# An attention and MLP kernel: two rows of a weight product in float32, group scores merged, zeros moved to the front

## The chip, the cores and the metric

The kernel runs on one core of a Trainium2 chip. The metric is the device time of one execution in microseconds (us), the median of several runs. A core has these engines: TensorE (PE; its weight loads are listed as PEld), VectorE (DVE), ScalarE (ACT), GpSimd (POOL) and SyncE (SP), which issues most transfers.

## What is computed

```python
q_d = q.reshape(B, H, Sd, factor, D).mean(axis=3)      # k_d, v_d alike; factor 4
out_up = np.repeat(sm_attn(q_d, k_d, v_d), factor, axis=2)
mask = np.abs(pos[:, None] - pos[None, :]) < factor
scores = np.where(mask, scale * np.matmul(q, k.transpose(0, 1, 3, 2)), -1e9)
out_local = softmax(scores) @ v
x = (out_up + out_local).transpose(0, 2, 1, 3).reshape(B * S, H * D)
return ((x @ w1) * (x @ w2)) @ w3 @ w_out
```

B = H = 8, S = 576, D = 64; x is 4608 x 512, w1 and w2 are 512 x 1024, w3 is 1024 x 1024, w_out 1024 x 512. The four weights arrive as 64-bit floats, everything else is float32.

## The kernel before

**The weight product.** The last two weights are multiplied once on the chip (`fold`): w3 @ w_out, 1024 x 512, stays in `wphl`. w3 is cut into blocks of 128 rows of the inner dimension, j = 0 to 7, and two halves mq of four output blocks m. A block row j needs block j of w_out (`out_weight`) and block (j, mq) of w3 (`block`); `product(m, j)` adds their product to the sum of m, which stays in PSUM until j = 7, and `keep` stores it.

**Split float32.** A float32 product is computed by `three` as three float32r instructions: high x high, high x low, low x high. Every operand is therefore split into a high part (a copy by ACT) and a low part (a subtraction by DVE). A weight block goes through `words` and `parted`: SP loads the 64-bit words (L337, 512 KB); ACT makes the upper part (L344); the low bits come from ACT (L352) or DVE (L356, "shift"); DVE joins them (L359, "join"); ACT copies the high half (L371); DVE subtracts (L375).

**Attention.** Batches 0 and 1 do the local attention on PE in groups of 16 pooled positions: for each unit n (a third of a batch) `group_scores` computes scores of two quads of heads (L769, tile `se_ps`), adds the band mask (L780), takes the maximum (L789, L790), exponentials on ACT (L793) and normalises; `group_values` multiplies by v. Batches 2 to 7 do it on DVE and ACT (`unit`). The pooled attention of each batch (`pooled`, `quad`) gives scores `s_ps`, transposes `t_ps` and values `o_ps` on PE. `pooled_sums` loads q and k in four phases for batches 0 and 1, sums them and turns q into natural order.

**The chunks.** Two units form a chunk of 384 rows of x. `moe(c)` computes, for eight blocks f of 128 features, the two gate products (tile `pab`, 24 instructions for each), multiplies them (ACT and DVE, then split into `gh`, `gl`), and three down products (`acc`, three instructions each) with `wphl`.

**What sets the order.** All work is a list of tasks with an engine, a cost and dependencies. The table ORDER names, for each engine, the order of its tasks; `Plan.order` interleaves the engines by those costs, and each engine then runs its own queue strictly in that order. A ring (`R[...]`) of n buffers makes a task wait until the one n places before has been used up; the small PSUM tiles of the scores and transposes share one ring of three ("g").

At the start, `warm` multiplies zeros (`still`, L412) on PE, 20 times, before the first product.

Of the kernel before, what the change touches and what calls it, by code (L numbers as in the profile page):

```python
# [20 lines left out]
FAC = 4  # L21
# [31 lines left out]
            g=2, o=2, ab=2, acc=1, ps=3, p=1, pt=1, oup=2, vs=1, qks=1, x=2, s=3, gs=3, q4=2, k4=2, qn=2, vw=4, se=4, pte=1, xf=1)  # L53
# [4 lines left out]
WARM = 20  # L58
# [41 lines left out]
    ),  # L100
    DVE=(
# [62 lines left out]
    ),  # L164
)

LOWS = dict(early=('ACT', 'ACT', 'DVE'), late=('ACT', 'DVE'))


class Ring:  # L170
# [91 lines left out]
def mm_us(n):  # L262
    return n * 0.43e-3 + 0.0095
# [10 lines left out]
def tile_attention_moe(ctx: ExitStack, tc: tile.TileContext, q, kw, vw, qk4, v4, w1, w2, w3, wout, edge, out):  # L274
# [115 lines left out]
    def fold():  # L390
# [66 lines left out]
        for mq in range(2):  # L457
            for j in range(NF):
                if not mq:
                    out_weight(j)  # L460
# [763 lines left out]
```

## Time and profile before

| | |
|---|---|
| median of three runs | 750.81 us (749.66 to 752.25) |
| profiled execution: span, first to last instruction | 747.4 us |
| PE busy | 729.4 us (98%) |
| DVE busy | 617.8 us (83%) |
| ACT busy | 544.3 us (73%) |
| POOL busy | 108.2 us (14%) |
| HBM read, written | 80.26 MB, 9.44 MB |

The span is that of one profiled execution; its own whole time is not listed beside it, and the median of the runs lies 3.4 us above the span. Busy times are unions over the span. A PE instruction's end is modelled and reaches into the next one, so the pace is read from starts. Names with numbers such as `wo_302` are tiles; before, a line of `three` is L312, L313 or L314, after the change L316, L317 or L318.

### The profile page before, as it was taken

The numbers are of one execution on the slowest core, as the hardware profiler recorded it, in microseconds if no ns is written. First come the engines' busy times: TensorE is split into PE (matmuls) and PEld (weight loads), VectorE is DVE, ScalarE is ACT, GpSimd is POOL, SyncE is SP. The second block draws the span as 40 slices with busy tenths as digits, with TensorE's granted clock in tenths as the row PEclk, the third lists the DMA queues.
The fourth block names the chain that finished last, engine by engine and source line by source line (L and its number), as shares of the span: only waits on it lengthen the run. The fifth ranks groups of instructions, "written<-read, shape, count | busy, mean of one in ns | idle before, by whom it ended". The sixth has DMA issues, their size and how long they took to land.

```text
span 747.4 us, 15049 instructions
## 1 busy us (share of the span) xinstructions
PE 729.4 (98%) x5352; PEld 658.2 (88%) x5352; DVE 617.8 (83%) x1088; ACT 544.3 (73%) x2157; POOL 108.2 (14%) x139
## 2 busy tenths in 40 slices
PE   4999999999999999999999999999999999999997
PEld 3677888789998989999898998999899999999996
DVE  6988996557999999989999998999989988885212
ACT  5999878566897878778878886877887875853211
POOL 2020002210112210212222110221120110010000
PEclk9999999999999999999999999999999999999999
DMA  8998765746767877396577674668666354233101
GB/s 257 322 261 262 236 204 105 131 84 194 151 143 175 167 171 189 61 241 165 89 168 220 120 184 150 100 197 176 141 145 164 63 152 127 63 66 56 43 0 43
DMA packets 51999, 111.91 MB, mean 150 GB/s; under 512 B 5060, under 2 KB 19396, under 8 KB 51924
## 3 DMA queue, kind: packets, MB, share of 16 engines
q0 software_dynamic: 14592, 38.94, 30.9%
q1 hardware_dynamic: 37044, 71.74, 29.0%
q8 instruction: 42, 0.69, 0.4%
q10 hardware_dynamic: 288, 0.27, 0.1%
q14 instruction: 33, 0.27, 0.1%
HBM read 80.26 MB, written 9.44 MB: 120 GB/s over the span
## 4 chain that ended last, share of the span: by engine, by line
PE 96%; DVE 2%; DMA 1%; issue 0%; ACT 0%; SPq 0%
PE pab L312 19%; PE pab L314 18%; PE pab L313 18%; PE acc L312 9%; PE acc L313 9%; PE acc L314 9%; PE o_ps L553 2%; PE accw L312 2%; PE s_ps L592 2%; PE t_ps L631 2%; PE accw L313 2%; PE accw L314 2%; PE se_ps L769 1%; PE oe_ps L812 1%; PE te_ps L739 1%; DMA q<-in_qk_dram 1%
## 5 line engine op out<-in xcount | busy, mean ns | idle before, releaser
L942 ACT ACTIVATE pv<-kv,s 128x64 f32<-128x64 f32 x432 | 115.3, 338 | 15.2 <-DVE s L919 8.9
L894 ACT ACTIVATE junk<-pr 128x64 f32<-128x64 f32 x432 | 110.2, 255 | 17.3 <-DVE pr L884 8.0
L884 DVE TENSOR_TENSOR pr<-q_t,kv 128x768 f32<-128x768 f32 x126 | 115.8, 950 | 0.6 <-ACT junk L894 0.3
L312 PE MATMUL acc<-wphl,gh 128*128 128x512 f32 x288 | 113.6, 395 | 0.0
L314 PE MATMUL acc<-wphl,gl 128*128 128x512 f32 x288 | 112.9, 392 | 0.0
L313 PE MATMUL acc<-wphl,gh 128*128 128x512 f32 x288 | 112.8, 392 | 0.0
L958 POOL DMA_DIRECT2D xl<-pv x54 | 46.5, 862 | 370.2 <-DVE xl L960 271.3
L1047 DVE TENSOR_TENSOR a<-pab,a 128x384 f32<-128x384 f32 x96 | 53.1, 553 | 45.1 <-PE pab L314 35.2
L1045 ACT COPY a<-pab 128x384 f32<-128x384 f32 x96 | 45.3, 471 | 60.4 <-PE pab L314 56.3
L897 DVE TENSOR_REDUCE s<-pr 128x12 f32<-128x768 f32 x90 | 83.8, 946 | 0.4
L894 ACT ACTIVATION_READ_ACCUMULATOR junk<-pr 128x1 f32 x432 | 81.1, 188 | 0.0
L1052 ACT CAST gh<-a 128x384 fp32r<-128x384 f32 x96 | 48.9, 510 | 38.5 <-PE acc L313 27.5
L1054 DVE TENSOR_TENSOR gl<-a,gh 128x384 fp32r<-128x384 f32 x96 | 52.7, 552 | 26.8 <-ACT gh L1052 26.5
L950 DVE TENSOR_TENSOR pv<-kv,s 128x768 f32<-128x768 f32 x72 | 67.7, 951 | 0.4
L312 PE MATMUL pab<-xh,w1a 128*128 128x384 f32 x192 | 65.7, 342 | 0.0
L312 PE MATMUL pab<-xh,w2a 128*128 128x384 f32 x192 | 65.4, 340 | 0.0
L312 PE MATMUL pab<-xh,wo 128*128 128x384 f32 x192 | 65.3, 340 | 0.0
L312 PE MATMUL pab<-xh,wb 128*128 128x384 f32 x192 | 65.2, 339 | 0.0
L314 PE MATMUL pab<-xh,wo 128*128 128x384 f32 x192 | 64.5, 336 | 0.0
L314 PE MATMUL pab<-xh,wb 128*128 128x384 f32 x192 | 64.5, 336 | 0.0
L314 PE MATMUL pab<-xh,w1a 128*128 128x384 f32 x192 | 64.5, 336 | 0.0
L313 PE MATMUL pab<-xl,wo 128*128 128x384 f32 x192 | 64.5, 336 | 0.0
(126 smaller groups left out, 1766.6 us busy)
## 6 DMA issues: line engine op xcount, KB each, us to landing
xl<-pv POOLq DMA_DIRECT2D x54, 384.0 KB, 4.2
raw<-in_w_dram SPq DMA_DIRECT2D x32, 512.0 KB, 5.3
qks<-in_qk_dram POOLq DMA_DIRECT2D x18, 576.0 KB, 7.3
kv<-in_kw_dram SPq DMA_DIRECT2D x18, 576.0 KB, 4.1
kv<-in_vw_dram SPq DMA_DIRECT2D x18, 576.0 KB, 5.5
q_t<-in_q_dram SPq DMA_DIRECT2D x18, 384.0 KB, 3.3
vs<-in_v_dram POOLq DMA_DIRECT2D x24, 256.0 KB, 5.7
out_dram<-o_sb SPq DMA_DIRECT2D x23, 256.0 KB, 2.8
```

The costliest lines, as they stand in the source:

```text
L312: nc.tensor.matmul(out_ps, lhsT=lh, rhs=rh, start=first, stop=False)
L313: nc.tensor.matmul(out_ps, lhsT=lh, rhs=rl, start=False, stop=False)
L314: nc.tensor.matmul(out_ps, lhsT=ll, rhs=rh, start=False, stop=last)
L884: (nc.gpsimd if o in share["qk_pool"] else nc.vector).tensor_tensor(out=T[o], in0=T["q"], in1=T["k"][:, o * D:o * D + nq].rearrange("p (t ...
L894: nc.scalar.activation(out=junk, in_=T[o][:, t], func=AF.Copy, accum_out=T["s"][:, t, o:o + 1])
L897: reds.append(add("DVE", dve_us(nq), lambda o=o: nc.vector.tensor_reduce(out=T["s"][:, :, o], in_=T[o], op=ALU.add, axis=AX.X), [tp], uses ...
L942: nc.scalar.mul(out=T["pv", o][:, tt], in_=T["v"][:, (tt + o) * D:(tt + o + 1) * D], mul=T["s"][:, tt, o:o + 1])
L950: nc.vector.tensor_tensor(out=T["pv", o], in0=T["v"][:, o * D:o * D + nq].rearrange("p (t d) -> p t d", d=D), in1=T["s"][:, :, o].unsqueez ...
L958: t = add("Pool", 0.9, lambda o=o: nc.gpsimd.dma_start(out=T["x"], in_=T["pv", o], accum_op=ALU.add), [t, tm], uses=[hx, h], late=dma_us(1 ...
L1047: tg = add("DVE", dve_us(CT), lambda f=f: nc.vector.tensor_tensor(out=straight(T["a", f]), in0=turned(T["p", 1, f]), in1=straight(T["a", f ...
L1052: nc.scalar.copy(out=T["gh", f], in_=T["a", f])
L1054: tl = add("DVE", dve_us(CT), lambda f=f: nc.vector.tensor_tensor(out=T["gl", f], in0=T["a", f], in1=T["gh", f].bitcast(F32), op=ALU.subtr ...
```

## The change

1. `WHOLE = (0, 1)`: the block rows j = 0 and 1 of the weight product are not split. Their four w3 blocks and two w_out blocks stay float32 (`whole`), and `product` multiplies them with one float32 instruction instead of three float32r ones. The two w_out blocks live in the `oup` buffers, and are the first weights to be loaded.
2. `group_scores` handles both quads of a unit in one task: 24 products, masks of 432, a maximum of 864 elements; `pooled_sums` loads q and k of two head pairs at a time (`q4` has one buffer).
3. The band mask is moved by four products with the identity on PE (`banding`, L686) and one DVE copy, not by eight DVE copies; with the zeros, now 26, it stands first on PE.
4. `NORM_DVE = (0,)`: for batch 0 the pooled probabilities are normalised by DVE (two operations a quad), not by ACT.
5. ORDER is new for all engines.

```diff
-            g=2, o=2, ab=2, acc=1, ps=3, p=1, pt=1, oup=2, vs=1, qks=1, x=2, s=3, gs=3, q4=2, k4=2, qn=2, vw=4, se=4, pte=1, xf=1)
+            g=2, o=2, ab=2, acc=1, ps=3, p=1, pt=1, oup=2, vs=1, qks=1, x=2, s=3, gs=3, q4=1, k4=2, qn=2, vw=4, se=2, pte=1, xf=1)
-WARM = 20
+WARM = 26
+NORM_DVE = (0,)
+WHOLE = (0, 1)
...
+    def whole(src, parts, place, take=()):
+        T, ld, tx, h = words(src, place, list(take), "early", parts)
+        early.append(tx)
+        return T, [tx], h
...
     def out_weight(j):
...
+        if j in WHOLE:
+            T, wo_ready[j], wo_held[j] = whole(wout[j].unsqueeze(1), 1, lambda: work.tile([128, KT * SD], F32, name="oup", bufs=BUFS["oup"])[:, :DM], [R["oup"]])
+            wo_whole[j] = T
+            return
...
         def block(j, mq):
...
+            if j in WHOLE:
+                xs[j, mq] = whole(src, 4, lambda: pools["early"].tile([128, nw], F32, name="wx", bufs=BUFS["early_wx"]), [R["early_wx"]])
+                return
...
-                three(accs[m], T["h"][:, cs], T["l"][:, cs], wo[0][:, j], wo_low[:, j], j == 0, j == NF - 1)
+                if j in WHOLE:
+                    nc.tensor.matmul(accs[m], lhsT=T["x"][:, cs], rhs=wo_whole[j]["x"], start=j == 0, stop=j == NF - 1)
+                else:
+                    three(accs[m], T["h"][:, cs], T["l"][:, cs], wo[0][:, j], wo_low[:, j], j == 0, j == NF - 1)
...
+        if b in NORM_DVE:
+            for par in range(2):
+                no.append(add("DVE", dve_us(nt * width[par]), lambda par=par: nc.vector.tensor_tensor(out=T["of"][par][:, :, :width[par]], in0=T["of"][par][:, :, :width[par]], in1=wide_(T["sm"][:, :nt, par], width[par]), op=ALU.mult), [rs], uses=[hg, hp]))
+        for par, i in slots if b not in NORM_DVE else ():
...
+    def banding():
...
+                for i, (at, n) in enumerate(((0, 2), (1, 2))):
+                    nc.tensor.matmul(T["b"][rows, 2 * i:2 * i + n], lhsT=ident[rows, rows], rhs=masks[0][rows, half, at:at + n].rearrange("p i s f -> p (i s f)"), start=True, stop=True)
...
-    def group_scores(b, j, qd, starts):
+    def group_scores(b, j, starts):
...
+                U["s", par] = ps.tile([128, 2, NG, GK], F32, tag="g", name="se_ps", bufs=BUFS["ps"])
+            for qd in range(2):
+                for g, (q0, k0) in enumerate(starts):
...
-        sc, b0, b1 = add("PE", 2 * NG * mm_us(2 * GK) + SWITCH, score, l4, take=[R["ps"], R["ps"]], uses=h4)
+        sc, b0, b1 = add("PE", 4 * NG * mm_us(2 * GK) + SWITCH, score, sum(l4s, []), take=[R["ps"], R["ps"]], uses=sum(h4s, []))
...
+    for j in WHOLE:
+        out_weight(j)
```

The queue of PE at its start, before (`se_ps` are group scores, `still` the zeros, `accw` the sums of the weight product):

```order
L769 MATMUL se_ps<-k_153,qn 64x72 x12
L412 MATMUL accw_197<-still 128x128 x20
L312 MATMUL accw_197<-wo,w_178 128x512
L313 MATMUL accw_197<-wphl,w_178 128x512
L314 MATMUL accw_197<-wo,w_178 128x512
```

and with the change (`b_ps` is the band mask, L456 the float32 product, `s_ps` the pooled scores):

```order
L686 MATMUL b_ps<-xh_97,ident 64x144 x4
L429 MATMUL accw_146<-still 128x128 x26
L456 MATMUL accw_146<-oup,wx 128x512
L456 MATMUL accw_147<-oup,wx 128x512
L456 MATMUL accw<-oup,wx 128x512 x2
L456 MATMUL accw_148<-oup,wx 128x512
L796 MATMUL se_ps<-k_191,qn 64x72 x12
L796 MATMUL se_ps<-k_193,qn 64x72 x12
L456 MATMUL accw_148<-oup,wx 128x512
L456 MATMUL accw_146<-oup,wx 128x512
L456 MATMUL accw_147<-oup,wx 128x512
L796 MATMUL se_ps<-k_191,qn 64x72 x12
```

The zeros no longer stand behind the first group scores; eight float32 products and the scores of two units stand ahead of the first split product. The other eight float32 products stand behind the first half, in three places between split products.

The queue of DVE from the first group masks on, with the change (`wx` joins, `raw` shift, `emx` maximum, `wphl` and `w_320` the low halves for the first split product):

```order
L807 TENSOR_TENSOR se<-se_ps,band 128x432 x2
L363 SCALAR_TENSOR_TENSOR wx<-wx,raw 128x512
L360 TENSOR_SCALAR raw<-raw 128x512
L817 TENSOR_REDUCE emx<-se 128x12
L818 TENSOR_SCALAR emx<-emx 128x12
L363 SCALAR_TENSOR_TENSOR wx<-wx,raw 128x512
L380 TENSOR_TENSOR wphl<-wx,wo 128x512
L807 TENSOR_TENSOR se<-se_ps,band 128x432
L363 SCALAR_TENSOR_TENSOR wx<-wx,raw 128x512
L380 TENSOR_TENSOR w_320<-wx,w_320 128x512
```

Before, the low halves of the first split product stand ahead of the first group masks:

```order
L1149 COPY band<-xh_97 64x72 x8
L375 TENSOR_TENSOR wphl<-wx,wo 128x512
L375 TENSOR_TENSOR w_178<-wx,w_178 128x512
L700 TENSOR_TENSOR qks<-k_153 128x288
L780 TENSOR_TENSOR se<-se_ps,band 128x216 x2
```

So the masks of both units, and with them the PE tasks that they wait for, now stand on DVE ahead of the halves that the first split product needs.

PE at the last group scores before the gates, before:

```order
L769 MATMUL se_ps<-k_153,qn 64x72 x12
L312 MATMUL accw<-wo,w_911 128x512
L313 MATMUL accw<-wphl,w_911 128x512
L314 MATMUL accw<-wo,w_911 128x512
L769 MATMUL se_ps<-k_272,qn 64x72 x12
L312 MATMUL pab<-xh_984,w1a 128x384
```

and with the change:

```order
L316 MATMUL accw_582<-wo,w_784 128x512
L317 MATMUL accw_582<-wphl,w_784 128x512
L318 MATMUL accw_582<-wo,w_784 128x512
L796 MATMUL se_ps<-k_191,qn 64x72 x12
L796 MATMUL se_ps<-k_193,qn 64x72 x12
L316 MATMUL pab<-xh_881,w1a 128x384
```

The two tasks of a unit have become neighbours; the other three units behind this place change in the same way. From the first gate on, the down products stand in 172 unbroken runs between gate products, before in 103.

## Rows read from the trace of the kernel before

**Rows 1.** The page's part 4: the chain that ended last, by engine.
```profile
PE 96%; DVE 2%; DMA 1%; issue 0%; ACT 0%; SPq 0%
```

**Rows 2.** Waits of PE from 28 us to the end.
```profile
PE se_ps L769 <- DVE se L780: 0.7, 1, 0.7
```

**Rows 3.** Timeline of PE, start: start us, us, engine, line, operation, tiles, shape [idle before].
```profile
11.10 1.03 PE L769 MATMUL se_ps<-k,qn 64*64 64x72 f32 x24 [11.10 <-DMA k<-in_qk_dram]
12.06 7.17 PE L412 MATMUL accw<-still 128*128 128x128 f32 x40
19.00 0.48 PE L312 MATMUL accw<-wo,w 128*128 128x512 f32 x1
...
21.11 0.40 PE L313 MATMUL accw<-wphl,w 128*128 128x512 f32 x1
22.21 0.50 PE L314 MATMUL accw<-wo,w 128*128 128x512 f32 x1 [0.70 <-DVE w L375]
```

**Rows 4.** Timeline of POOL, its last masks.
```profile
4.57 1.31 POOL L1146 TENSOR_SCALAR_AFFINE_SELECT xh<-xh 128x72 f32<-128x72 f32 x3
```

**Rows 5.** Zeros of L412 by stretch: us, busy us (records) of PE and PEld, PEclk, DMA, GB/s.
```profile
12.10:17.20 5.10, 5.10 (x24) 5.10 (x25) 1.00 0.74 233
```

**Rows 6.** Timeline of PE around a lone task of group scores.
```profile
30.00 0.40 PE L313 MATMUL accw<-wphl,w 128*128 128x512 f32 x1
30.23 0.39 PE L314 MATMUL accw<-wo,w 128*128 128x512 f32 x1
30.55 0.97 PE L769 MATMUL se_ps<-k,qn 64*64 64x72 f32 x24
31.45 0.50 PE L312 MATMUL accw<-wo,w 128*128 128x512 f32 x1
31.80 0.39 PE L313 MATMUL accw<-wphl,w 128*128 128x512 f32 x1
```

**Rows 7.** Timeline of DVE between 13 and 19 us.
```profile
13.45 0.67 DVE L780 TENSOR_TENSOR se<-se_ps,band 128x216 f32<-128x216 f32 x2
...
14.25 0.42 DVE L356 TENSOR_SCALAR raw<-raw 128x512 int32<-128x512 int32 x1
14.59 0.30 DVE L683 TENSOR_TENSOR qks<-qks,q 128x144 f32<-128x144 f32 x1
14.81 0.69 DVE L359 SCALAR_TENSOR_TENSOR wx<-wx,raw 128x512 int32<-128x512 int32 x1
15.41 0.60 DVE L789 TENSOR_REDUCE emx<-se 128x6 f32<-128x432 f32 x1
15.92 0.30 DVE L683 TENSOR_TENSOR qks<-qks,q 128x144 f32<-128x144 f32 x1
...
17.09 0.94 DVE L700 TENSOR_TENSOR qks<-qks,k 128x288 f32<-128x288 f32 x2
17.95 0.68 DVE L375 TENSOR_TENSOR wphl<-wx,wo 128x512 fp32r<-128x512 f32 x1
18.55 0.69 DVE L359 SCALAR_TENSOR_TENSOR wx<-wx,raw 128x512 int32<-128x512 int32 x1
```

**Rows 8.** All engines from 3 to 13 us; the last two columns are DMA share and GB/s.
```profile
3.00:13.00 10.00, 1.90 (x28) 1.77 (x29) 5.22 (x16) 4.24 (x7) 2.88 (x8) 1.00 1.04 353
```

**Rows 9.** Timeline of PE: three places of the run.
```profile
51.50 0.40 PE L312 MATMUL accw<-wo,w 128*128 128x512 f32 x1
...
83.65 0.44 PE L312 MATMUL pab<-xh,w1a 128*128 128x384 f32 x1
...
741.14 0.39 PE L314 MATMUL acc<-wphl,gl 128*128 128x512 f32 x1
...
741.82 0.39 PE L314 MATMUL acc<-wphl,gl 128*128 128x512 f32 x1
```

**Rows 10.** Timeline of PE: a lone run of three down instructions.
```profile
181.84 0.39 PE L312 MATMUL acc<-wphl,gh 128*128 128x512 f32 x1
...
182.53 0.34 PE L312 MATMUL pab<-xh,wo 128*128 128x384 f32 x1
```

More of the change, by code (lines that the diff above doesn't have):

```diff
@@ L299, in tile_attention_moe @@
     nc.vector.memset(soft[:, :, SD:KEYS[1]], 0.0)
-    bands = []
+    bands, masks, band_sb = [], [], []
     gates = [[wpool.tile([128, KT, 2, 512], F32R, name=f"w{w}a"), None, None] for w in (1, 2)]
@@ L363, in tile_attention_moe @@
     wo_ready, wp_ready, g_ready = {}, {}, {}
+    wo_whole, wo_held = {}, {}
     wo_low = wphl[:, NF // 2:].rearrange("p f h n -> p (f h) n")
@@ L445, in product @@
             else:
-                t = add("PE", 3 * mm_us(DM), prod, deps, uses=[h, held[m]])
+                t = add("PE", 3 * mm_us(DM), prod, deps, uses=[h, held[m]] + wh)
             last[m] = t
@@ L458, in fold @@
             for j in range(NF):
-                if not mq:
+                if not mq and j not in WHOLE:
                     out_weight(j)
@@ L653, in pooled_sums, with turn @@
     @plan.named
+    def banding():
+        T = {}
+        def turn():
+            T["b"] = ps.tile([128, NG + 1, GK], F32, tag="g", name="b_ps", bufs=BUFS["ps"])
+            for half in range(2):
+                rows = slice(half * GQ, half * GQ + GQ)
+                for i, (at, n) in enumerate(((0, 2), (1, 2))):
+                    nc.tensor.matmul(T["b"][rows, 2 * i:2 * i + n], lhsT=ident[rows, rows], rhs=masks[0][rows, half, at:at + n].rearrange("p i s f -> p (i s f)"), start=True, stop=True)
+        t, bank = add("PE", 0.8, turn, take=[R["ps"]])
+        t = add("DVE", dve_us(4 * GK), lambda: nc.vector.tensor_copy(out=band_sb[0], in_=T["b"]), [t], uses=[bank])
+        pep.append(t)
+        return t
+    banded = banding()
+    @plan.named
     def pooled_sums(b):
@@ L658, in pooled_sums @@
         for qd in range(2):
-            fours[b][qd] = {}
-            tq = hn = None
-            for w in range(2):
-                x = {}
-                def load_q(qd=qd, w=w, x=x):
-                    x["q"] = pools["pep"].tile([128, FAC, SD], F32, name="q4", bufs=BUFS["q4"])
-                    nc.sync.dma_start(out=x["q"], in_=qk4[b, :, :, 0, 2 * qd + w].rearrange("f p s -> p f s"))
-                lq4, hq4 = add("SP", 0.5, load_q, take=[R["q4"]], late=dma_us(128 * 2304))
-                def turn(qd=qd, w=w, x=x):
-                    if w == 0:
-                        fours[b][qd][0] = pools["pep"].tile([128, 2, SD, FAC], F32, name="qn", bufs=BUFS["qn"])
-                    nc.vector.tensor_copy(out=fours[b][qd][0][:, w], in_=x["q"].rearrange("p f s -> p s f"))
-                if w == 0:
-                    tq, hn = add("DVE", dve_us(4 * SD), turn, [lq4], take=[R["qn"]], uses=[hq4])
-                else:
-                    tq = add("DVE", dve_us(4 * SD), turn, [lq4, tq], uses=[hq4, hn])
-                t = lq4
+            x = fours[b][qd] = {}
@@ new lines, in turn @@
+            def turn(x=x):
+                x["n"] = pools["pep"].tile([128, 2, SD, FAC], F32, name="qn", bufs=BUFS["qn"])
+                nc.vector.tensor_copy(out=x["n"], in_=x["q"].rearrange("p f w s -> p w s f"))
+            lq4, hq4 = add("SP", 0.5, load_q, take=[R["q4"]], late=dma_us(128 * 4608))
+            tq, hn = add("DVE", dve_us(8 * SD), turn, [lq4], take=[R["qn"]], uses=[hq4])
+            lk4, hk4 = add("SP", 0.5, load_k, take=[R["k4"]], late=dma_us(128 * 4608))
+            for i, (nm, t, h4) in enumerate((("q", lq4, hq4), ("k", lk4, hk4))):
@@ L678, in pooled_sums, with total @@
                 for f in range(1, FAC):
-                    def total(qd=qd, f=f, w=w, x=x):
-                        if qd == w == 0 and f == 1:
+                    def total(qd=qd, f=f, i=i, nm=nm, x=x):
+                        if qd == i == 0 and f == 1:
                             raws.setdefault(b, {})[0] = work.tile([128, 2, NQ, SD], F32, name="qks", bufs=BUFS["qks"])
-                        to = raws[b][0][:, 0, 2 * qd + w]
-                        nc.vector.tensor_tensor(out=to, in0=x["q"][:, 0] if f == 1 else to, in1=x["q"][:, f], op=ALU.add)
+                        to = raws[b][0][:, i, 2 * qd:2 * qd + 2]
+                        nc.vector.tensor_tensor(out=to, in0=x[nm][:, 0] if f == 1 else to, in1=x[nm][:, f], op=ALU.add)
@@ L684, in pooled_sums @@
                     if hq is None:
-                        t, hq = add("DVE", dve_us(SD), total, [t], take=[R["qks"]], uses=[hq4])
+                        t, hq = add("DVE", dve_us(2 * SD), total, [t], take=[R["qks"]], uses=[h4])
                         first = t
                     else:
-                        t = add("DVE", dve_us(SD), total, [t, first], uses=[hq4, hq])
+                        t = add("DVE", dve_us(2 * SD), total, [t, first], uses=[h4, hq])
                 done.append(t)
-                pep.extend([lq4, tq])
@@ L692, in load_k @@
-            def load_k(qd=qd):
-                x = fours[b][qd][1] = pools["pep"].tile([128, FAC, 2, SD], F32, name="k4", bufs=BUFS["k4"])
-                nc.sync.dma_start(out=x.rearrange("p f w s -> p f (w s)"), in_=qk4[b, :, :, 1, 2 * qd:2 * qd + 2].rearrange("f p w s -> p f (w s)"))
-            lk4, hk4 = add("SP", 0.5, load_k, take=[R["k4"]], late=dma_us(128 * 4608))
-            t = lk4
-            for f in range(1, FAC):
-                def total(qd=qd, f=f):
-                    to, x = raws[b][0][:, 1, 2 * qd:2 * qd + 2], fours[b][qd][1]
-                    nc.vector.tensor_tensor(out=to, in0=x[:, 0] if f == 1 else to, in1=x[:, f], op=ALU.add)
-                t = add("DVE", dve_us(2 * SD), total, [t, first], uses=[hk4, hq])
@@ L702, in pooled_sums @@
-            done.append(t)
-            pep.append(lk4)
+            pep.extend([lq4, tq, lk4])
             four_ready[b].append(([tq, lk4], [hn, hk4]))
@@ L727, in group_unit @@
         pep.extend(lvs)
-        quads = [group_scores(b, j, qd, starts) for qd in range(2)]
+        U, hs, no = group_scores(b, j, starts)
         @plan.named
@@ L756, in group_scores @@
     @plan.named
[L757 removed]
+    def group_scores(b, j, starts):
         U = {}
[L760 removed]
+        l4s, h4s = zip(*four_ready[b])
         def score():
             for par in range(2):
[L764 to L770 removed]
+                U["s", par] = ps.tile([128, 2, NG, GK], F32, tag="g", name="se_ps", bufs=BUFS["ps"])
+            for qd in range(2):
+                for g, (q0, k0) in enumerate(starts):
+                    for w in range(2):
+                        for par in range(2):
+                            qs, ks = (fours[b][qd][i][par * D:par * D + D] for i in "nk")
+                            nc.tensor.matmul(U["s", par][w * GQ:w * GQ + GQ, qd, g], lhsT=qs[:, w, q0:q0 + GS].rearrange("p s f -> p (s f)"), rhs=ks[:, :, w, k0:k0 + WS].rearrange("p f s -> p s f"), start=True, stop=True)
+        sc, b0, b1 = add("PE", 4 * NG * mm_us(2 * GK) + SWITCH, score, sum(l4s, []), take=[R["ps"], R["ps"]], uses=sum(h4s, []))
         pep.append(sc)
@@ L776, in mask @@
                 if par == 0:
-                    U["p"] = pools["pep"].tile([128, 2, NG, GK], F32, name="se", bufs=BUFS["se"])
+                    U["p"] = pools["pep"].tile([128, 2, 2, NG, GK], F32, name="se", bufs=BUFS["se"])
                     for nm in ("mx", "sm"):
-                        U[nm] = pools["pep"].tile([128, 2 * NG], F32, name="e" + nm, bufs=BUFS["se"])
-                nc.vector.tensor_tensor(out=U["p"][:, par], in0=U["s", par], in1=bands[j].rearrange("p g s f -> p g (s f)"), op=ALU.add)
+                        U[nm] = pools["pep"].tile([128, 4 * NG], F32, name="e" + nm, bufs=BUFS["se"])
+                nc.vector.tensor_tensor(out=U["p"][:, par], in0=U["s", par], in1=bands[j].unsqueeze(1).to_broadcast([128, 2, NG, GK]), op=ALU.add)
             if hs is None:
-                t, hs = add("DVE", dve_us(NG * GK), mask, [sc], take=[R["se"]], uses=[bank])
+                t, hs = add("DVE", dve_us(2 * NG * GK), mask, [sc, banded], take=[R["se"]], uses=[bank])
             else:
-                t = add("DVE", dve_us(NG * GK), mask, [sc] + msk, uses=[bank, hs])
+                t = add("DVE", dve_us(2 * NG * GK), mask, [sc] + msk, uses=[bank, hs])
             msk.append(t)
-        n2 = 2 * NG * GK
-        p3 = lambda: U["p"].rearrange("p a s k -> p (a s) k")
-        wide_ = lambda x: x.unsqueeze(2).to_broadcast([128, 2 * NG, GK])
+        nb = 4 * NG
+        n2 = nb * GK
+        p3 = lambda: U["p"].rearrange("p a d s k -> p (a d s) k")
+        wide_ = lambda x: x.unsqueeze(2).to_broadcast([128, nb, GK])
         t = add("DVE", dve_us(n2), lambda: nc.vector.tensor_reduce(out=U["mx"], in_=p3(), op=ALU.max, axis=AX.X), msk, uses=[hs])
@@ L791, in group_scores @@
         ex = []
-        for i in range(2 * NG):
+        for i in range(nb):
             ex.append(add("ACT", act_us(GK, 2), lambda i=i: nc.scalar.activation(out=p3()[:, i], in_=p3()[:, i], func=AF.Exp, bias=U["mx"][:, i:i + 1], scale=1.0 / D ** 0.5, accum_out=U["sm"][:, i:i + 1]), [t], uses=[hs]))
@@ L1135, in tile_attention_moe @@
         left[side] = set(l[0][0])
[L1138 removed]
+    band = pools["pep"].tile([128, NG + 1, GK], F32, name="band")
     for both in [work.tile([128, KT, CT], F32R, name="xh0", bufs=1).rearrange("p k t -> p (k t)")[:, :6 * GK].bitcast(F32).rearrange("p (h i s f) -> p h i s f", h=2, i=3, f=FAC)]:
@@ L1146, in tile_attention_moe @@
                 nc.gpsimd.affine_select(out=at, in_=at, compare_op=ALU.is_ge, fill=-8e9, base=HALO - off - GQ * half, pattern=[[-FAC, WS], [-1, FAC]], channel_multiplier=1)
-        for half in range(2):
-            for i in range(NG + 1):
-                nc.vector.tensor_copy(out=band[half * GQ:half * GQ + GQ, i], in_=both[half * GQ:half * GQ + GQ, half, 0 if i == 0 else 2 if i == NG else 1])
-    bands.extend([band[:, :NG], band[:, 1:2].to_broadcast([128, NG, WS, FAC]), band[:, 1:]])
+        masks.append(both)
+    bands.extend([band[:, :NG], band[:, 1:2].to_broadcast([128, NG, GK]), band[:, 1:]])
+    band_sb.append(band)
     with tc.manual_schedule():
```

29 lines of the change are left out of this document (13 added, 16 removed), and 184 rows, old and new, of tables (ACT, DVE, PE, Pool).

## The prediction

> **What bounds the kernel now.** I read the chain of waits first: its share by engine says that TensorE ends it nearly alone [rows 1]. Then the waits of PE alone: from 28 us to the end it waits once for another engine, 0.7 us [rows 2]. So every microsecond after 28 us is PE's own instruction stream, and only three things can move the end: when the stream begins, how long its instructions take, and whether a new wait gets in.
>
> Then the first 29 us of PE in the timeline [rows 3]. PE does nothing until the first group scores (11.10), runs 20 multiplications of zeros (12.06) and begins the weight product at 19.00. It then stands 0.87 us before L314 at 22.21 (1.10 from the start before it less that one's own 0.23) and 0.7 us at 28.06 [rows 2]; with small ones some 2 us up to there. It waits for DVE, which makes the low halves of the weights. The change puts the zeros first, lets float32 products run that need no halves, and merges the group scores.
>
> **Zeros first.** The masks that the new first PE task reads are finished by POOL at 5.88 [rows 4]; I let PE begin at 5.9. Its four small matrix products take about as long as the 24 records of group scores did at that point (0.96 us, 11.10 to 12.06 [rows 3]); I take 1.2, so the 26 zeros begin at 7.1. The pace of the zeros doubles on the way: 24 records (12 zeros, two records each) lie in the 5.1 us up to 17.2, which is 0.427 us for a zero; the other 16 lie between there and 19.00, 0.225 us for one [rows 3, 5]. The clock column shows 1.00 (2.4 GHz) even for the first stretch, yet its pace is half the later one, that of the lower level of 1.2 GHz; PE had worked without a gap from 11.10 to 17.2. If it rises as long after PE's first work as it did here, that is at 12.0: 11.5 zeros at 0.427, 14.5 at 0.225, and the first product stands at **15.3** in place of 19.00. Bounds: all zeros at the quick pace 12.9, all at the slow one 18.2.
>
> **Price of a float32 product.** Before, one product is three float32r instructions of 512 columns, each 0.233 apart (30.00 to 30.23 [rows 6]): 0.70 us. Sixteen of them become one float32 product of 512 columns, which no row shows. A zero has 128 columns in float32: four times the quick 0.225 is 0.90, and four times half of the slow 0.427 is 0.85 [rows 3, 5]. These are the bounds; I take 0.88, since the quick zeros are the nearest row and whatever an instruction costs at its start is paid once here, not four times. That is +0.18 for each product, **+2.9 us** for sixteen. The Trainium skill, FP8 and Floating Point Precision, section TensorE Precision Notes, speaks against this part: true float32 makes four passes through the array, so four passes stand here against three. The trace agrees (two records of twice the time for a zero); by the rule alone a product would cost 4/3 of 0.70, 0.93, and the sixteen 3.7 us.
>
> **The first 50 us, in order.** What runs early is set by DVE, so I walk along its queue with starts from the timeline [rows 7]: join 0.60 (14.81 to 15.41), subtraction 0.60 (17.95 to 18.55), shift 0.34 (14.25 to 14.59), mask of 216 elements 0.30 (two in 0.67, of which the last tenth overlaps), maximum over 432 elements 0.51 (15.41 to 15.92), sum of 288 elements 0.43 (two from 17.09 to 17.95). The doubled forms come from these: mask of 432 0.53, maximum of 864 0.97, short ones 0.12.
> - Loads: 0.59 MB of q, four blocks of 0.52 MB and three of 0.59 MB come ahead of the scores, 4.5 MB. At the 353 GB/s of 3 to 13 us [rows 8] the last lands near 16. PE needs it at 19.7, so the rate could fall to 270 GB/s and the load would stay hidden.
> - PE: five float32 products from 15.3 to 19.7. Then the merged scores. A lone task of 24 records occupies 0.90 (30.55 to 31.45 [rows 6]); the way in costs 0.09 (0.32 from L314 to the scores against 0.23) and the way out 0.11 (0.34 to L313). The inner part of 24 records is 0.76, so 48 take 1.52. They end near 21.4.
> - DVE then does two masks, join, shift, maximum, scale, join, subtraction: 4.3 us to 25.7. Meanwhile PE runs three products and the next scores, done near 25.8; mask, join and subtraction follow, and the low half of the first split block is there at 27.6. PE, ready for it near 26.5 (after the pooled scores, whose bank is free only after that mask), starts L318 at 27.7.
> - To the low half of the next block DVE has two maxima over 288 elements (0.37 each, between the 0.51 for 432 and the 0.30 for 216), join, shift, scale, mask, subtraction, join, subtraction: 4.1 us, 31.7. PE has finished four products at 30.0 and starts that L318 at 31.8, over a microsecond late. It has done these four at 34.1 and three of the next at 36.2.
> - There stand the transposes of the pooled scores. In the change DVE also normalises these scores for this batch (two operations of 256 and 288 elements, 0.37 and 0.40), behind three joins, two subtractions, the long maximum, a shift and three short steps: 5.5 us, 37.2. PE waits another 1.0 and then has cover: thirteen products, 9.1 us, the transposes 0.75 and the second pooled scores 1.25, to **48.4**.
> Before, PE is as far at 51.50, less two products of the next half already done, 1.4: **50.1** [rows 9]. Gain at this point **1.7 us**: 3.7 from the earlier beginning and 2.2 of waits removed, less 3.5 of new waits and 1.4 for the first eight dearer products; the rest is fewer ways in and out.
>
> **From there on.** Eight float32 products +1.44. They stand in three places between split ones, and each way out costs 0.11: +0.32. One pair of scores merged before the gates: two lone tasks cost 2 x 1.10, a merged one 1.82, so -0.38. The first gate product then starts at 83.65 - 1.7 + 1.44 + 0.32 - 0.38 = **83.3** [rows 9].
> After it PE works 658.2 us without a wait to the last matmul (83.65 to 741.82 [rows 9]). Three more merged pairs give -1.15. Against them, gates and down products are cut finer: the down products stand in 172 runs, not 103. A lone run of three takes 0.69 (181.84 to 182.53 [rows 10]) where three in a long run take 0.68 (741.14 to 741.82 [rows 9]); with the gates behind it, slower by about the same again, some 0.016 us for each of 69 runs, **+1.1**. Bounds 0 and 1.5. Sum after the gates: 0.
> The tail (last matmul to the end, 5.6 us) has the same instructions. DVE and ACT work that is dropped (six subtractions and six copies) lies under PE after 28 us and gives nothing by itself.
>
> **Sum:** -0.3 us at the gates, 0 behind: span 747.4 - 0.3 = 747.1. The median of the runs, 750.81, lies 3.4 above this span; I add the same: **750.5**. A measurement of this kernel can tell about 0.3% from no change, 2.25 us (748.56 to 753.06).
>
> **The rivals.**
> Faster: DVE keeps up and the 3.5 us of new waits do not come, because the steps that I set end to end overlap. For it: before, PE never waits for DVE after 28.06 [rows 2], though DVE is busy 83% of the span. Against it: 864-element steps and masks now stand ahead of the joins. Time: 750.5 - 3.5 = 747.0.
> Slower, one mechanism: PE's pace stays at the lower level through the zeros, as the little products ahead of them leave PE partly idle. It decides if more than 22 of the 26 zeros run slow (start later than 17.5). Then the products begin at 18.2, the scores, the masks and everything on DVE behind them 2.9 later: 753.4. For it: 12 zeros were slow here. Against it: the rise came under just such zeros.
> Slower, elsewhere: with down products cut finer, a product follows its low half on DVE more closely, and PE waits in the gates' stretch. Before has 44 lone runs without one wait. Three us of such waits: 753.5.
> The change does not do what it says: a float32 product costs what the split one does. Then -2.9: 747.6. The zeros speak against it.
>
> **How the numbers follow.** My forecast, within 0.3%: 0.52, float32 priced anywhere within its bounds (0.8 us) included. DVE keeps up: 0.25, a cheaper product 0.05; both faster, 0.30. Zeros slow 0.08, waits in the gates' stretch 0.10: slower, 0.18. The range must reach both 747.0 and 753.5; beyond lie combinations of two cases: 746.8 to 753.5.
>
> **What would show it.** Right: the first float32 product near 15.3, two records of about 0.44 each; PE idle of 1 us or more before L318 near 28 and 32 and before the transposes near 37, released by DVE; 48 score records in about 1.6; first gate near 83.3; no PE wait behind it. Wrong: zeros that end after 17.5, a float32 product under 0.8, PE without idle after 20 us, or rows of waits released by DVE's low halves after 84 us.

## The result and the profile after

| | before | changed |
|---|---|---|
| median of the runs | 750.23 us (749.16 to 752.25) | 755.33 us (754.40 to 756.72) |
| ratio, 95% interval | | 1.0071 (1.0051 to 1.0091) |
| profiled execution: span | 747.4 us | 753.3 us |
| first gate product | 83.65 us [rows 9] | 82.22 us |
| last matmul | 741.82 us [rows 9] | 747.51 us |
| from one to the other | 658.2 us | 665.3 us |
| PE, DVE, ACT busy | 729.4, 617.8, 544.3 us | 737.2, 606.7, 537.6 us |

The changed kernel is slower by 0.7%, 5 us; the forecast was 750.5 us, with a range up to 753.5. The table says where to look: up to the first gate product the change gained 1.4 us, and behind it it lost 7.1. (The spans differ by 5.9 us, the medians by 5.1: the median lies 2.0 us above the span here, where the forecast added 3.4.) The chain of waits (page, part 4), 96% PE before [rows 1], now passes through four others:

```profile
PE 78%; DVE 8%; issue 5%; DMA 5%; POOL 1%; ACT 1%; SPq 0%; POOLq 0%; DVEq 0%; ACTq 0%
```

The waits of PE from 84 us to the end (engine, what waits, releaser; total us, times, longest), which were none before [rows 2]:

```profile
PE pab L316 <- DVE a L1075: 2.2, 2, 1.2
PE pab L316 <- ACT a L1073: 0.9, 1, 0.9
PE oe_ps L840 <- DMA v_w<-in_v_dram: 0.5, 1, 0.5
PE pab L317 <- DVE raw L360: 0.4, 1, 0.4
PE te_ps L765 <- DVE se L824: 0.4, 1, 0.4
```

They sum to 4.4 us. A wait costs some more than it lists, since a PE instruction's modelled end hides a part of it. I therefore also compared every interval between the starts of neighbouring PE instructions with the mean of the same pair, at the same place of its run, in the kernel before. What an interval has above that mean is called its excess below. Seven pieces of excess are 0.25 us or more; they stand before 84.12 (0.58), 88.15 (1.08), 105.73 (0.57), 165.90 (0.67), 388.94 (1.36), 512.59 (0.31) and 580.04 us (1.21) and sum to 5.8 of the 7.1 us. With small pieces too I first put the sum at 7.2, the number used in two expectations below; but that sum hangs on how small a piece still counts (6.4 us for those above 0.1 us, 9.2 for those above 0.08), so it doesn't show that all of the loss is waits.

The largest piece, in the timelines of PE and of DVE (start us, us, engine, line, operation, tiles, shape, [idle before, releaser]):

```profile
387.12 0.39 PE L317 MATMUL acc<-wphl,gh 128*128 128x512 f32 x1
387.35 0.40 PE L318 MATMUL acc<-wphl,gl 128*128 128x512 f32 x1
388.94 0.45 PE L316 MATMUL pab<-xh,w2a 128*128 128x384 f32 x1 [1.19 <-DVE a L1075]
```

```profile
384.86 0.96 DVE L912 TENSOR_TENSOR pr<-q_t,kv 128x768 f32<-128x768 f32 x1
385.74 0.95 DVE L925 TENSOR_REDUCE s<-pr 128x12 f32<-128x768 f32 x1
386.60 0.95 DVE L978 TENSOR_TENSOR xl<-kv,s 128x768 f32<-128x768 f32 x1
387.47 0.95 DVE L978 TENSOR_TENSOR pv<-kv,s 128x768 f32<-128x768 f32 x1
388.33 0.55 DVE L1075 TENSOR_TENSOR a<-pab,a 128x384 f32<-128x384 f32 x1
```

PE could begin the next gate product at 387.6. The tile `pab` has two buffers in PSUM (the accumulator memory that PE writes), and the one it needs is emptied by the DVE multiplication L1075. That multiplication could have run earlier, as e4 below shows, but it stands in DVE's queue behind two attention products of 0.87 us each. DVE is not idle here; the multiplication is late because of its place in the queue.

### The profile page after: what moved, and what is told of

It reads as the page before. It is cut to its first block, busy times and chain, and to the rows that moved or that the text cites. A ratio compares the mean times of both kernels' runs of the same rounds, so it can differ in the third digit from the quotient of the medians.

```text
span 753.3 us, 14941 instructions
## 1 busy us (share of the span) xinstructions
PE 737.2 (98%) x5356; PEld 657.5 (87%) x5356; DVE 606.7 (81%) x1021; ACT 537.6 (71%) x2141; POOL 108.8 (14%) x139
## 4 chain that ended last, share of the span: by engine, by line
PE 78%; DVE 8%; issue 5%; DMA 5%; POOL 1%; ACT 1%; SPq 0%; POOLq 0%; DVEq 0%; ACTq 0%
PE pab L316 15%; PE pab L318 14%; PE pab L317 14%; PE acc L316 7%; PE acc L317 7%; PE acc L318 7%; DMA xl<-pv 3%; PE accw L456 2%; PE o_ps L574 2%; DMA raw<-in_w_dram 1%; PE t_ps L655 1%; PE s_ps L613 1%; DVE pr L912 1%; PE accw L429 1%; PE accw L316 1%
## 5 line engine op out<-in xcount | busy, mean ns | idle before, releaser
L970 ACT ACTIVATE pv<-kv,s 128x64 f32<-128x64 f32 x432 | 118.3, 338 | 20.2 <-DVE s L947 19.1
L912 DVE TENSOR_TENSOR pr<-q_t,kv 128x768 f32<-128x768 f32 x126 | 117.6, 950 | 3.3 <-DMA q_t<-in_q_dram 2.6
L318 PE MATMUL acc<-wphl,gl 128*128 128x512 f32 x288 | 113.4, 394 | 0.0
L1075 DVE TENSOR_TENSOR a<-pab,a 128x384 f32<-128x384 f32 x96 | 52.9, 551 | 46.6 <-PE pab L318 39.4
L978 DVE TENSOR_TENSOR pv<-kv,s 128x768 f32<-128x768 f32 x72 | 68.0, 951 | 0.0
L316 PE MATMUL pab<-xh,w1a 128*128 128x384 f32 x192 | 65.6, 342 | 0.9 <-ACT a L1073 0.9
L316 PE MATMUL pab<-xh,wo 128*128 128x384 f32 x192 | 65.2, 339 | 0.1
L317 PE MATMUL pab<-xl,w1a 128*128 128x384 f32 x192 | 64.5, 336 | 0.4 <-DVE raw L360 0.4
L318 PE MATMUL pab<-xh,wb 128*128 128x384 f32 x192 | 64.6, 337 | 0.0
L317 PE MATMUL pab<-xl,wb 128*128 128x384 f32 x192 | 64.6, 336 | 0.0
```

The lines of the kernel that those rows point to most:

```text
L316: nc.tensor.matmul(out_ps, lhsT=lh, rhs=rh, start=first, stop=False)
L317: nc.tensor.matmul(out_ps, lhsT=lh, rhs=rl, start=False, stop=False)
L318: nc.tensor.matmul(out_ps, lhsT=ll, rhs=rh, start=False, stop=last)
L912: (nc.gpsimd if o in share["qk_pool"] else nc.vector).tensor_tensor(out=T[o], in0=T["q"], in1=T["k"][:, o * D:o * D + nq].rearrange("p (t ...
L970: nc.scalar.mul(out=T["pv", o][:, tt], in_=T["v"][:, (tt + o) * D:(tt + o + 1) * D], mul=T["s"][:, tt, o:o + 1])
L978: nc.vector.tensor_tensor(out=T["pv", o], in0=T["v"][:, o * D:o * D + nq].rearrange("p (t d) -> p t d", d=D), in1=T["s"][:, :, o].unsqueez ...
```

## The experiments

**Theory:** the loss behind the first gate product is made by the new table ORDER, which puts gate copies and multiplications behind attention work; edits 1 to 4 make none of it. **Rivals:** the edits, or an earlier PE, cause the waits in any sequence; or the float32 products cost more than their length.

All numbers on one line of this table come from one profiled execution, but for the ratio, which compares its runs with runs of the kernel before on the same chip. Four groups ran together: e1 to e4, e5 to e7, e8 to e10, and e11 with e12. The changed kernel itself has 1.0071 in the runs of the result and 1.0108 as e10, so a difference of 0.4% between lines of different groups decides nothing. Nor is the profiled execution always a middle one: that of e10 is the slowest of its four runs (759.40 us), those of e4 and e11 are the fastest of theirs (754.84 and 748.27).

| run | ratio to before (95%) | first gate | first gate to last matmul | listed PE waits in it |
|---|---|---|---|---|
| before | 1 | 83.65 | 658.2 | 0 |
| changed | 1.0071 (1.0051 to 1.0091) | 82.22 | 665.3 | 4.4 |
| e10 changed again | 1.0108 (1.0093 to 1.0122) | 84.43 | 667.3 | 5.0 |
| e3 before, new sequence late | 1.0098 (1.0073 to 1.0122) | 83.88 | 665.6 | 3.5 |
| e1 changed, old sequence late | 1.0053 (1.0036 to 1.0071) | 84.75 | 661.4 | 2.6 |
| e8 as e1, gate stretch reordered too | 1.0043 (1.0031 to 1.0055) | 84.53 | 660.0 | 0.6 |
| e4 changed, four tasks moved | 1.0104 (1.0080 to 1.0128) | 83.56 | 663.6 | 2.8 |
| e5 changed, all engines reordered | 1.0146 (1.0126 to 1.0167) | 91.36 | 661.8 | 2.1 |
| e2 before, float32 alone | 1.0010 (1.0000 to 1.0021) | 84.65 | 658.6 | 0.2 |
| e7 changed, 14 zeros | 1.0047 (1.0032 to 1.0062) | 82.40 | 662.2 | 2.2 |
| e6 as e5, 14 zeros | 1.0118 (1.0096 to 1.0139) | 90.40 | 662.7 | 1.0 |
| e9 as e8, 14 zeros | 1.0012 (1.0003 to 1.0021) | 81.20 | 661.9 | 2.5 |
| e11 as e9, more lead | 0.9994 (0.9982 to 1.0007) | 80.64 | 660.0 | 0.7 |
| e12 as e11, 10 zeros | 0.9990 (0.9978 to 1.0002) | 82.27 | 659.6 | 0.2 |

**The sequence alone (e3, e1).** e3 puts the new sequence into the kernel before, e1 the old one into the changed kernel, both in the late part only. The edit is a rearranged ORDER of all five engines, so PE's own finer runs change together with the queues of the others; at the place shown above, DVE's rows in the changed kernel (-) and in e1 (+):

```diff
 L978 TENSOR_TENSOR xl<-kv,s_80 128x768
-L978 TENSOR_TENSOR pv<-kv,s_80 128x768
 L1075 TENSOR_TENSOR a<-pab,a 128x384
+L912 TENSOR_TENSOR pr<-q_t,kv 128x768 x3
+L925 TENSOR_REDUCE s_81<-pr 128x12
+L1075 TENSOR_TENSOR a<-pab,a 128x384
 L1082 TENSOR_TENSOR gl<-a,gh 128x384
+L978 TENSOR_TENSOR pv<-kv,s_80 128x768
```

> The kernel before, none of the edits, but the units from the fifth on and the chunks from the third on stand in the changed kernel's sequence. Theory: PE waits appear behind DVE and ACT tasks where the changed kernel has them in that part, 1.36 + 0.31 + 1.21 = 2.9 us, up to 3.6 with what stands beside them: 753.1 to 753.8, first gate at 83.65 as before. Rival (the sequence is harmless, the edits or the earlier PE make the waits): 750.2.

> The changed program whole (float32 products, zeros first, merged scores), but the tasks of the second batch's pooled attention, of the units behind the group attention and of the chunks of gate and down products from the second on stand on every engine in the sequence of the kernel before. Theory: the loss is made by the new sequence, so the four waits of the changed kernel that lie there (0.67 us at 165.90, 1.36 at 388.94, 0.31 at 512.59, 1.21 at 580.04) go and the ones at 84 to 106 us (0.58, 1.08, 0.57) stay; 755.3 - 3.5 = 751.8, first gate product at 82.2 as in the changed kernel. Rival (an earlier PE and the edits themselves make PE overrun DVE, whatever the sequence): waits of some 3 us come back at other places, 755.

e3 came out at 756.39 us against 749.61, +6.8, with none of the edits. Its waits, and DVE and PE at the largest (L950 and L1047 are here what L978 and L1075 are in the changed kernel):

```profile
PE pab L312 <- DVE a L1047: 2.2, 2, 1.1
PE s_ps L592 <- ACT oup L566: 0.8, 1, 0.8
PE pab L312 <- ACT a L1045: 0.3, 1, 0.3
PE t_ps L631 <- ACT pexp L620: 0.2, 1, 0.2
```

```profile
388.41 0.95 DVE L950 TENSOR_TENSOR xl<-kv,s 128x768 f32<-128x768 f32 x1
389.27 0.95 DVE L950 TENSOR_TENSOR pv<-kv,s 128x768 f32<-128x768 f32 x1
390.14 0.55 DVE L1047 TENSOR_TENSOR a<-pab,a 128x384 f32<-128x384 f32 x1
```

```profile
389.23 0.40 PE L314 MATMUL acc<-wphl,gl 128*128 128x512 f32 x1
390.75 0.45 PE L312 MATMUL pab<-xh,w2a 128*128 128x384 f32 x1 [1.12 <-DVE a L1047]
```

It is the changed kernel's row for row: the same wait, behind the same two products, 1.8 us later. The other large ones are at 581.24 (1.28), where the changed kernel has 580.04, and at 227.07 us (1.06), where it has none. The rival that needs the edits falls. The size was underestimated (+6.8 for 2.9 to 3.6). The pieces of 0.25 us or more sum to 4.7 of the 7.4 us by which the stretch is longer. The other 2.7 us lie in small waits and in the down products, which this sequence cuts into more runs; the two are not told apart.

e1 is the other half. Behind 175 us it has no piece of 0.25 us or more (2.9 us in the changed kernel): 388.94, 512.59 and 580.04 are gone, as forecast. The time, 753.78, is 2 us above the theory's value, and the trace shows that the part ahead did not stay: the first gate came at 84.75, 2.5 us later than in the changed kernel's first trace, and 1.67 us at 90.76, 0.60 at 155.56 and 0.91 at 168.26 stood in the rest.

**The rest of the stretch (e8, with e10 as control).** e8 starts from e1's sequence. Between 80 us and the third chunk it orders some DVE, ACT and PE tasks anew; it also moves single DVE and ACT tasks further behind, up to 661 us, which its expectation does not name. Two rows of DVE as an example:

```diff
-L360 TENSOR_SCALAR raw<-raw 128x512
-L1075 TENSOR_TENSOR a<-pab,a 128x384
+L1075 TENSOR_TENSOR a<-pab,a 128x384
+L360 TENSOR_SCALAR raw<-raw 128x512
```

> The run with the late sequence of the kernel before, and in the stretch from 80 us to the third chunk some DVE, ACT and PE tasks in another order too (gate copies and multiplications, transposes' copies and group scores further ahead); loads as there, zeros and everything ahead of the first gate product unchanged. Theory: the waits that were left at 90.76 (1.67), 155.56 (0.60) and 168.26 us (0.91) are places in queues as well and go by 2 of their 3.2 us: 2 us under that run, 0.2 to 0.3% above the kernel before. Rival (they come from the merged scores' longer steps or from transfers): no change against that run, 0.5% above the kernel before.

e10 is the changed kernel, with no edit, on the same chip.

> The changed kernel once more, nothing changed, on the chip of these runs. Theory: its waits stand at the same tasks, and their lengths vary with the landing of transfers from one execution to the next (the run with 14 zeros had none at 166, 512 and 580 us and the same first gate product): 753 to 756. Rival (that run's lower time came from its zeros): 755.3.

The control took 757.30 us, e8 752.24, with the same instructions and the first gate at 84.43 and 84.53. Their PE waits from 84 us on, first e10, then e8:

```profile
PE oe_ps L840 <- DMA v_w<-in_v_dram: 2.0, 1, 2.0
PE pab L316 <- ACT a L1073: 1.8, 2, 1.5
PE pab L316 <- DVE a L1075: 1.0, 1, 1.0
PE pab L317 <- DVE xl L858: 0.2, 1, 0.2
```

```profile
PE te_ps L765 <- DVE se L824: 0.4, 1, 0.4
PE te_ps L765 <- DVE xf L849: 0.2, 1, 0.2
```

So sequence alone takes 5.1 us out of the time, and 7.3 out of the stretch of these two executions, of which e10's is a slow one. The merged scores and the other edits leave room enough near 84 to 170 us. e8 is 0.43% above before, e1 was 0.53%: the forecast gain of 2 us on e1 shows in the waits (2.6 to 0.6), hardly in the time. e8's stretch is still 1.8 us longer than that of the kernel before, with 0.6 us of listed waits; that edits 1 to 4 cost nothing there is shown no closer than this. The control also shows what a single trace hides: the waits at 90.81 (1.62), 169.59 (2.21) and 394.23 (1.21) are those of the first trace at 88.15, 165.90 and 388.94, with other lengths; those at 512 and 580 are missing. At 169.59 the values (`v_w`) landed late. Its median lies above the expected 753 to 756. In its profiled execution the first gate comes 2.2 us later than in the first trace and the stretch is 2.0 us longer; the later start is in the zeros, see below.

**One task at a time (e4).**

```diff
 L925 TENSOR_REDUCE s_81<-pr 128x12
+L1075 TENSOR_TENSOR a<-pab,a 128x384
 L978 TENSOR_TENSOR xl<-kv,s_80 128x768
 L978 TENSOR_TENSOR pv<-kv,s_80 128x768
-L1075 TENSOR_TENSOR a<-pab,a 128x384
...
```

> The changed kernel; only four tasks are moved up in their queues: the DVE multiplication of gate (5, 1) ahead of two products of a unit, that of gate (8, 5) ahead of three steps of attention, the ACT copy of gate (7, 4) ahead of products, the ACT copy of gate (0, 0) ahead of two low words. Theory: each PE wait is the place of one task in one queue, so 1.36 + 1.21 + 0.31 + 1.08 = 4.0 us go, 751.3. Rival (DVE has no slack, a wait comes back at what was put behind): 754 to 755, with new waits of the same size within some 10 us of each move.

The rival was nearer: 757.23 us (754.84 to 760.16), no gain. The trace is of the fastest run. In it the four waits went, and others came: 0.69 at 90.60, 0.45 at 93.25, 0.87 at 169.66, 0.49 at 620.49, and close to the first move this one, behind an ACT copy of the gate (PE, then ACT):

```profile
391.18 0.34 PE L318 MATMUL pab<-xh,w2a 128*128 128x384 f32 x1
392.37 0.44 PE L316 MATMUL pab<-xh,w1a 128*128 128x384 f32 x1 [0.85 <-ACT a L1073]
```

```profile
390.53 0.46 ACT L662 COPY pt<-t_ps 128x384 f32<-128x384 f32 x1
390.88 0.58 ACT L1098 COPY o_sb<-acc 128x512 f32<-128x512 f32 x1
391.36 0.59 ACT L970 ACTIVATE pv<-kv,s 128x64 f32<-128x64 f32 x2
391.85 0.47 ACT L1073 COPY a<-pab 128x384 f32<-128x384 f32 x1
```

This copy was not moved: it stands behind the same copies and attention products in the changed kernel, where it ended at 391.81 and PE came to this product at 392.17. Now PE would be there at 391.36, and ACT runs 0.5 us later. A wait is thus the place of a task, but mending places one by one passes it on to the next. Why the median is 2.4 us above the traced run, the trace can't say.

**Transfers count too (e5).** e5 starts from e1's sequence and moves tasks on all five engines, SP's loads among them; three of its rows:

```diff
+L341 DMA raw<-in_wout_dram 128x1024
+L341 DMA raw<-in_w_dram 128x4x256 x5
 L538 DMA vs<-in_v_dram 128x512
```

> The changed program whole, same instructions; only the sequence of the tasks on the five engines is another: a gate's ACT copy and DVE multiplication stand further ahead of attention work, group values and loads have more lead. Theory: the loss is the sequence alone, in the stretch from 82 to 207 us too, so the PE waits behind the first gate product fall from 7.2 us to under 2: 755.3 less 5 to 7, 748.3 to 750.3. Rival (the merged scores and doubled steps leave DVE and ACT too little room near 84 to 170 us in any sequence): waits of 3 us and more stay there, 752 or more.

It was the slowest, 761.10 us. Behind the gate the stretch shrank (661.8; listed waits 2.1, and by excess 3.3 us where the theory gave under 2), but six weight blocks stand ahead of the value load, and the pooled values waited for it:

```profile
PE o_ps L574 <- DMA vs<-in_v_dram: 5.3, 1, 5.3
PE pab L317 <- DVE wphl L475: 1.1, 1, 1.1
```

The 5.3 us lie ahead of the first gate, which came at 91.36. The run has a fault of its own and decides nothing on the sequence behind the gate; from e8 on SP's and POOL's order stayed as in e1.

**Float32 alone (e2).** The kernel before in its own order; only this:

```diff
-                three(accs[m], T["h"][:, cs], T["l"][:, cs], wo[0][:, j], wo_low[:, j], j == 0, j == NF - 1)
+                if j in WHOLE:
+                    nc.tensor.matmul(accs[m], lhsT=T["h"][:, cs].bitcast(F32), rhs=wo[0][:, j].bitcast(F32), start=j == 0, stop=j == NF - 1)
```

> The kernel before in its own sequence; only the sixteen products of each half with the first two blocks are one float32 instruction each on the rounded high half, so what the low halves add for these blocks is left out of the result, while DVE and ACT still make them. Theory: 16 x (0.876 - 0.70) = +2.8 us on PE; the waits for the low halves near 22 and 28 us (0.87 and 0.70) may go, -1.6; no wait behind the first gate. 750.2 + 2.8 - 1.6 = 751.4, at most 753.0. Rival (the float32 products are the loss, by more than their length): 755 or more.

750.43 against 749.61 us, +0.8, and the first gate 1.0 later. By their length the products are dearer by 2.8 us. The first of them came 0.55 us earlier than before and the 0.87 us at the low half near 22 us are gone; what else made up for the rest was not traced. The stretch behind is 658.6. The rival falls.

**Fewer zeros (e7, e9, e6).**

```diff
-WARM = 26
+WARM = 14
```

> The changed kernel in its own sequence, 14 zeros in place of 26 and nothing else. Theory: first gate product about 2 us earlier, but behind it PE waits for tasks of DVE and ACT whose times do not depend on PE's start, so half or more of it is given back: 754 to 755, PE waits behind the first gate above 7.2 us. Rival (the waits are lengths of their own, a start that is 2 us earlier is an end 2 us earlier): 753.2.

> The same with 14 zeros in place of 26. Theory: as in the changed kernel with 14 zeros, PE runs 2 us ahead up to 58 us and has given it back by the first gate product, since ACT, filled with weight words that wait for their transfers, sets the pace from there: the same time as with 26 zeros, within 0.5 us. Rival (the earlier start is lost only to waits behind the gates): 2 us less.

> The same, with 14 zeros in place of 26. Theory: the changed kernel's DVE stood idle for 2.17 us before 20.39 because PE reached the merged scores late; its joined words were there at 11.17. Twelve quick zeros less take 12 x 0.22 = 2.6 us out of PE before the first product, DVE's idle time goes, and the first gate product comes about 2 us earlier than in the run with 26 zeros; without waits behind it the end follows: 746.3 to 748.3. Rival (the masks' steps on DVE or the loads bound the start, or PE's pace falls back to the slow one): under 0.5 us at the first gate.

My theory was wrong in e7 and e9, the rivals were nearer. e9 is 749.78 us, 2.5 less than e8 on the same chip; its first gate came 3.3 us earlier. e7, against the control, is 0.6% nearer to before; its first gate, 82.40, stands where the first trace of the changed kernel has it, so a part of its gain lies in waits that did not come (2.2 us listed, against 4.4 and 5.0). e6 gains 1.0 at the first gate, as the load still holds it (4.8 us). The traces say why twelve zeros less can be worth more than the expected 2 us: their length is not fixed. In the control and in e9:

```profile
7.15 8.89 PE L429 MATMUL accw<-still 128*128 128x128 f32 x52
15.88 1.45 PE L456 MATMUL accw<-oup,wx 128*128 128x512 f32 x3
```

```profile
6.44 4.67 PE L429 MATMUL accw<-still 128*128 128x128 f32 x28
10.95 4.53 PE L456 MATMUL accw<-oup,wx 128*128 128x512 f32 x10
```

The first float32 product stood at 14.21 in the first trace of the changed kernel, at 15.88 in the second. With 14 zeros it stands at 10.95 (e9), 11.57 (e11), 12.04 (e7) and 13.03 (e6).

**Both together (e11, e12).** e11 gives more tasks of DVE and ACT lead over e9, in the way of e8; its PE queue is that of e9. e12 sets WARM to 10.

> As the run with 14 zeros and the other sequence in the gate stretch, with some DVE, ACT and PE tasks from 45 us on given more lead again (gate multiplications near 107 and 474 us, transposed probabilities' copies). Theory: its waits at 104.19 (1.03) and 474.07 us (1.34) are places in queues too and go: 2 us less, that is 0.1 to 0.2% under the kernel before. Rival (they move on to the next task, as with the four moves): the same as that run, 0.1% above the kernel before.

> The same with 10 zeros in place of 14. Theory: with 14 the first product stood at 10.95 to 12.04, its second operand is joined by DVE at 10.5 to 11.2, so ten zeros end before the data is there and the start no longer moves: within 0.5 us of the run with 14. Rival (PE needs the zeros for its quick pace: with fewer the float32 products run at the slow one): the first gate product 2 us or more later.

749.26 and 749.10 us against 749.57: the same as before, 1.1% to 1.2% under the control by the two ratios. e11's two waits went by half or more (0.26 left at 102.45, 0.65 at 471.47), so theory and rival each have a share. With ten zeros the first product stands at 11.45, against 11.57, so the time was forecast rightly, but not for the reason given. PE in e12:

```profile
7.12 4.50 PE L429 MATMUL accw<-still 128*128 128x128 f32 x20
11.45 4.46 PE L456 MATMUL accw<-oup,wx 128*128 128x512 f32 x10
```

DVE had joined the second operand at 10.65, and PE did not wait: all ten zeros ran at the slow pace (0.43 us each), and so ended where fourteen end when the quick pace begins under them. The float32 products behind ran as elsewhere (0.43 us a record), so the rival's mechanism did not come either; the first gate of this execution is 1.6 us later than e11's, which the medians do not show. No version beat the kernel before by more than the intervals tell.

## Why the prediction was wrong

- **Zeros first:** forecast start 7.1 and first product 15.3; measured 6.42 and 14.21, in the control 7.15 and 15.88. Right, within bounds of 12.9 and 18.2.
- **Price of a float32 product:** five took 4.38 us (14.21 to 18.59), 0.876 each with the way into the scores, 0.86 from start to start; forecast 0.88. Before they were 0.70 [rows 6]. The Trainium skill, FP8 and Floating Point Precision, section TensorE Precision Notes, gives four passes for true float32. Against three that would be 0.93, an estimate; the measurement decides.
- **DVE's chain:** 48 score records took 1.68 us with the way out (18.59 to 20.27; forecast 1.52 and 0.11). Of the three waits that were forecast, two came at their place. The first came just ahead of its place, at the pooled scores, and L318 at 26.71 waited for nothing:

```profile
18.59 1.75 PE L796 MATMUL se_ps<-k,qn 64*64 64x72 f32 x48
20.27 2.84 PE L456 MATMUL accw<-oup,wx 128*128 128x512 f32 x6
...
25.50 0.71 PE L613 MATMUL s_ps<-qks 64*64 64x144 f32 x14 [0.49 <-DVE se L807]
...
26.71 0.49 PE L318 MATMUL accw<-wo,w 128*128 128x512 f32 x1
...
30.85 0.50 PE L318 MATMUL accw<-wo,w 128*128 128x512 f32 x1 [0.70 <-DVE w L380]
...
36.66 0.66 PE L655 MATMUL t_ps<-ident,pexp 128*128 128x128 f32 x4 [0.74 <-DVE pexp L646]
```

  As listed they sum to 1.9 us. By starts, the measure of the prediction, they cost 0.76, 1.25 and 0.90, together 2.9 us against the 3.5 forecast. One reading of the kernel before was wrong there: its 0.7 us at 28.06 were not for a low half, but for a mask (`se`, [rows 2]). The first gate was forecast at 83.3 and came at 82.2 (84.4 in the control).
- **Merged pairs and finer runs behind the gates:** forecast -1.15 and +1.1, sum 0. From the start ahead of the scores to the start behind them, less the usual interval, a lone task costs 1.00 us (six before) and a merged one 1.77 (three after); with three ways out of 0.11 fewer the merged pairs give -1.0. Right. The large pieces (5.8) and this leave 2.3 of the 7.1 us for the finer runs and for small waits. That is above the bound of 1.5 for the finer runs; how much of it is theirs stays open.
- **The step that failed** is the sentence on which that sum stood, "After it PE works 658.2 us without a wait", carried over from the kernel before. It had no term for waits in the gates' stretch, where 5.8 of the 7.1 us came in seven places. The sequence of the kernel before keeps every gate copy and multiplication ahead of PE; "ORDER is new for all engines" was read for PE alone there. e3 shows that the kernel before, its queues replaced in that part, loses 6.8 us, and e8 that another sequence takes 5.1 us off the changed kernel. Not tried was PE's new queue with the other engines' old ones; that the place of a copy or multiplication makes the wait is read from the traces, from e4, which leaves PE's queue alone, and from e8, which moves three of its tasks against e1.
- **The rival that came** was "Slower, elsewhere", at a chance of 0.10. Its place was right, and its size (3 us) half of the seven pieces. Its mechanism was wrong: not a down product that meets its low half (no listed wait names `gl`), but a gate product whose PSUM buffer is emptied late. The evidence against it, 44 lone runs without one wait, belonged to a sequence that the change threw away.

## What to carry to other kernels

Where a change replaces the order of a kernel whose bound engine never waits, the absence of waits is not inherited: compare the queues of the engines that empty its PSUM buffers, task by task, and price every operation that moves ahead of such a task. Such waits move on when one task is moved, and their lengths differ between executions (0.5 and 2.0 us for the same wait on a load), so judge a sequence as a whole and from several executions. Work that only fills time at the start, such as zeros, should end when the first operands are there; here twelve fewer gave 2.5 us (e8 to e9), and four fewer still nothing.

## What was not expected of the hardware

**The zeros' pace rises at varying times, under a clock column of 1.00.** With the column at 1.00 (2.4 GHz) in every stretch, one zero (two records) takes 0.43 us at first and 0.22 later. In the changed kernel's two traces PE had worked from 3.33 us with short gaps and without one from 6.42 and 7.15; the quick pace began at 10.41 and 13.07. Stretches of the zeros' line in the control, ahead of and behind the rise (us, busy us and records of PE and PEld, PEclk, DMA share, GB/s):

```profile
7.20:12.90 5.70, 5.70 (x27) 5.70 (x28) 1.00 1.09 356
13.20:15.60 2.40, 2.40 (x24) 2.40 (x23) 1.00 1.09 380
```

Over the runs with zeros first it began between 9.16 (e9) and 13.07 us; in e12 not before the last zero, at 11.33. With the masks' end on POOL, 0.7 us apart in the two, this moves the first product of the same kernel by 1.7 us, nearly half of the 3.7 us that were forecast as won there; why it varies was not tried.

**Some of the sequences spread the time.** e4's six runs cover 754.84 to 760.16 us and e3's 755.21 to 761.38; the kernel before covers 748.44 to 752.28 in seventeen runs on that chip. One cause may be DVE's own waits for accumulated products (`xl<-pv`), with a gate multiplication behind them in its queue: 4.5 us in the changed kernel's first trace, 2.1 the longest and just ahead of the wait at 580, 1.6 in the control, 0.9 before. That these make the spread is argued, not shown: e4's trace has 1.5, no more than that of e8, whose runs cover only 751.08 to 752.99.
